# Strided attention heads on the 96-key blocks of the local heads: values on partitions 32 to 95

## Chip, cores and metric

One core of a Trainium2 chip runs the whole program in one launch. The metric is the time of one execution on the device in microseconds (us); the median of several runs is given, and beside it one execution that the profiler recorded.

## What is computed

The program is a causal sparse attention followed by two feed-forward stages (a mixture of experts with soft routing, then a gated layer). Only the attention is touched by the change:

```python
# B, H, S, D = 4, 8, 576, 64; stride 32
mask_local   = (rel >= 0) & (rel < stride)                            # heads 0 to 3
mask_strided = (rel >= 0) & (pos[None] % stride == pos[:, None] % stride)  # heads 4 to 7
scores = where(mask, scale * q @ k.T, -1e9);  attn = softmax(scores);  attn @ v
```

For a strided head the host stores the 576 positions in another order, residue by residue: 32 classes of 18 positions each. In that order a query sees only earlier keys of its own class of 18, so both kinds of head become a narrow band along the diagonal.

## The kernel before

**Units and tiles.** The attention is cut into 16 units, each a head for a pair of batch entries (`UNITS`, line 26). Their order is local, local, strided, strided, four times over, so units 2, 3, 6, 7, 10, 11, 14 and 15 are strided. A unit has nine query blocks of 64 rows. A local block looks at 96 keys (the 64 of its own block and the 32 before them), a strided one at 80 (the 64 and the 16 before). The widths are `WID = (96, 80)` on line 22; the key columns of a strided block begin 16 further on, by `SHIFT` on line 23.

**One unit.** `load_qk` (line 249) brings keys and queries, and `load_v` (line 254) the values: one DMA of 64 rows of 4680 bytes. It lands on partitions `W - 64` to `W`, that is 32 to 95 for a local head and 16 to 79 for a strided one. Then three copies on GpSimd (line 262) put the last `W - 64` rows of each block's predecessor onto partitions 0 to `W - 64`. The block's values are then `W` rows from partition 0. `qk` (line 274) makes the scores on TensorE (line 286); VectorE scales them, adds a mask (line 290) and takes the row maximum (line 291), in two parts of five and four blocks. `expo` (line 293) is the exponential on ScalarE, one instruction for each block. `tr` (line 298) transposes on TensorE (line 304) and copies on ScalarE (line 305). `pv` (line 307) multiplies with the values (line 321), and VectorE divides (lines 324 to 328). Every second unit, `xtr` (line 335) transposes the result again, and `logits` (line 345) multiplies it with the routing matrix.

**Order.** The order on each engine is written out by hand (line 594). Step n issues `qk(n)`, `tr(n-1)`, the exponentials of n, `pv(n-1)`, then the load of values n+1, then two weight loads of 512 KB each. Value tiles are two (`NV`), so the load of values n+1 waits for `pv(n-1)`; key tiles are three. All these loads are issued by SyncE and share one queue, so the packets of a load stand behind those of the loads issued before it. VectorE and ScalarE also convert some weights between the steps (`PRECONV`).

**Masks.** `h` is a piece of 96 columns of the constants' tile. `low` (line 525) fills it with two VectorE instructions; `cut` (line 517) compares it with a constant of each row and writes a mask in bf16. After step 0 `strided()` (line 534) fills `h` anew for 80 columns and makes the nine masks `ms` of the strided heads, before VectorE comes to the scores of unit 1. At about the same time GpSimd copies the values of unit 1 and zeroes the tile `eT` (line 544).

**After the attention** come the logits' end and the slots (lines 365 to 489), the expert layers (`w1_mm`, line 627, and line 719), for which the rest of the weights is loaded as buffers come free, and the gated layer (line 795 on).

Of the kernel before, what the change touches and what calls it, by code (L numbers as in the profile page):

```python
# [12 lines left out]
BF16 = mybir.dt.bfloat16  # L13
AF = mybir.ActivationFunctionType
ALU = mybir.AluOpType
# [3 lines left out]
HD = 64  # L19
NT = 9  # L20
PAD = 32
WID = (96, 80)
SHIFT = (0, 16)
NEG = -1.0e30
HORDER = (0, 1, 4, 5, 2, 3, 6, 7)
UNITS = [(bp, h) for bp in range(2) for h in HORDER]
# [49 lines left out]
def constants():  # L76
    p = np.arange(128)
    q = p % 64
    c = np.zeros((128, 16), np.float32)
    c[:, 0], c[:, 1], c[:, 2] = p, p % 32, p % 32 + 32 * (p // 64)  # L80
    c[:, 3], c[:, 4], c[:, 5], c[:, 15] = q, q + 32, q + 16, np.maximum(q, 31)
    for i in range(NT):
        c[:, 6 + i] = (64 * i + q) // 18 * 18 - 64 * i + 16
    return c


def layout(q, k, v, moe_phi, moe_w1, moe_w2, moe2_w_gate, moe2_w_val, moe2_w_out):
    pi = perm_index()
    kq = np.empty((16, 2, HD, 2, S), np.float32)
    vw = np.ones((16, 64, 2, NT, HD + 1), np.float32)  # L90
    for u, (bp, h) in enumerate(UNITS):
        y = h // 4
        o = pi if y else np.arange(S)
        kq[u, :, :, 0] = k[2 * bp:2 * bp + 2, h][:, o].transpose(0, 2, 1)
        kq[u, :, :, 1] = q[2 * bp:2 * bp + 2, h][:, o].transpose(0, 2, 1)
        vw[u, ..., :HD] = v[2 * bp:2 * bp + 2, h][:, o].reshape(2, NT, 64, HD).transpose(2, 0, 1, 3)
    w1 = moe_w1.reshape(8, 4, 128, 2, 512).transpose(0, 3, 2, 1, 4).reshape(16, 128, 2048)
    w2 = moe_w2.reshape(8, 2, 4, 128, 512).transpose(0, 1, 3, 2, 4).reshape(16, 128, 2048)
    g = bits(moe2_w_gate).reshape(4, 128, 12, 128)
    a = bits(moe2_w_val).reshape(4, 128, 12, 128)  # L100
    wgv = np.stack([g, a], axis=3).transpose(2, 1, 0, 3, 4).reshape(12, 128, 1024)
    wo = bits(moe2_w_out).reshape(6, 2, 128, 512).transpose(0, 2, 1, 3).reshape(6, 128, 1024)
    w1, w2 = (a.reshape(16, 128, 2, 1024).transpose(0, 2, 1, 3) for a in (w1, w2))
    wgv, wo = (a.reshape(-1, 128, 2, 512).transpose(0, 2, 1, 3) for a in (wgv, wo))
    phi = moe_phi.reshape(4, 128, 32).transpose(1, 0, 2).reshape(128, 128)
    arrs = dict(cst=constants(), phi=phi, kq=kq.reshape(16, 128, 2 * S),
                vh=vw.reshape(16, 64, -1),
                w1=w1, w2=w2, wgv=wgv, wo=wo)
    return {n: np.ascontiguousarray(x) for n, x in arrs.items()}
# [3 lines left out]
def build(ctx: ExitStack, tc: tile.TileContext, cst, phi, kq, vh, w1, w2, wgv, wo, out):  # L113
# [11 lines left out]
    lp = es_ld.enter_context(tc.tile_pool(name="ld", bufs=1, side="right"))  # L125
# [3 lines left out]
    def bank(tag, bufs):  # L129
        return pp[0].tile([128, 512], F32, tag=tag, name=tag, bufs=bufs)  # L130
# [17 lines left out]
    col = lp.tile([128, 128], F32, name="col")  # L148
    par = lp.tile([128, 16], F32, name="par")
    ml = lp.tile([128, 5, 96], BF16, name="ml")  # L150
    ms = lp.tile([128, 9, 80], BF16, name="ms")

    wsrc = [w1[j] for j in range(16)] + [w2[j] for j in range(16)]
    loads = [(j, hf) for j in PRE + WORDER for hf in range(2)]
# [99 lines left out]
    def load_v(u):  # L254
        if u >= 16:
            return
        W = WID[UNITS[u][1] // 4]
        t = vt[u % NV]
        SP.dma_start(out=t[W - 64:W], in_=vh[u])
        t4 = t.rearrange("p (b i d) -> p b i d", b=2, i=NT)  # L260
        for i0, i1 in ((1, 3), (3, 6), (6, 9)):
            POOL.tensor_copy(t4[0:W - 64, :, i0:i1, :], t4[64:W, :, i0 - 1:i1 - 1, :])  # L262

# [1 line left out]
    tmp = ap_.tile([128, 2880], F32, name="tmp")  # L265

    def etile(u):
        W = WID[UNITS[u][1] // 4]
        o = 864 * (u % 2)
        return tmp[:, o:o + NT * W].rearrange("p (j k) -> p j k", k=W)  # L270

    attile = tmp[0:96, 1728:2880].rearrange("p (j k) -> p j k", k=128)

    def qk(u):
        y = UNITS[u][1] // 4
        W = WID[y]
        e = etile(u)
        q, k = qbd[u % NQK], kt[u % NQK]
        mx = mxs[u] = ap_.tile([128, NT], F32, tag="mx", name="mx", bufs=2)
        for i0, i1 in zip(CUT, CUT[1:]):  # L280
            ps = bank("sc", 2)
            for i in range(i0, i1):
                c0 = 64 * i + SHIFT[y]
                for b in range(2):
                    h = slice(64 * b, 64 * b + 64)
                    PE.matmul(out=ps[h, W * (i - i0):W * (i - i0) + W], lhsT=q[h, 64 * i:64 * i + 64],  # L286
                              rhs=k[h, c0:c0 + W], start=True, stop=True, skip_group_check=True)
            p3 = ps[:, 0:(i1 - i0) * W].rearrange("p (j k) -> p j k", k=W)
            m3 = ms[:, i0:i1] if y else ml[:, i0:i1] if i0 == 0 else ml[:, 1:1 + i1 - i0]
            DVE.scalar_tensor_tensor(out=e[:, i0:i1], in0=p3, scalar=0.125, in1=m3, op0=ALU.mult, op1=ALU.add)  # L290
            DVE.tensor_reduce(out=mx[:, i0:i1], in_=e[:, i0:i1], axis=AX, op=ALU.max, negate=True)  # L291

    def expo(u, k):
        e, mx = etile(u), mxs[u]
        for i in range(CUT[k], CUT[k + 1]):
            ACT.activation(out=e[:, i], in_=e[:, i], func=AF.Exp, scale=1.0, bias=mx[:, i:i + 1])  # L296

    def tr(u):
        W = WID[UNITS[u][1] // 4]
        e = etile(u)  # L300
        for t in range(3):
            ps = bank("tr", 3)
            for j in range(3):
                PE.transpose(ps[0:W, 128 * j:128 * j + 128], e[:, 3 * t + j], ident)  # L304
            ACT.copy(attile[0:W, 3 * t:3 * t + 3], ps[0:W, 0:384].rearrange("p (j q) -> p j q", j=3))  # L305

    def pv(u):
        bp, h = UNITS[u]
        y = h // 4
        W = WID[y]  # L310
        st, e = divmod(h % 4, 2)
        if e == 0:
            xt[bp, y, st] = ap_.tile([128, NT, 128], F32, tag="x", name="x", bufs=6)
        x, v = xt[bp, y, st], vt[u % NV]
        dn = ap_.tile([128, 2, NT, 1], F32, tag="dn", name="dn", bufs=2)
        half = []
        for i0, i1 in zip(CUT, CUT[1:]):
            ps = bank("pv", 2)
            for i in range(i0, i1):
                for b in range(2):  # L320
                    PE.matmul(out=ps[64 * b:64 * b + 64, 65 * (i - i0):65 * (i - i0) + 65], lhsT=attile[0:W, i, 64 * b:64 * b + 64],  # L321
                              rhs=v[0:W, 65 * (NT * b + i):65 * (NT * b + i) + 65], start=True, stop=True, skip_group_check=True)
            p3 = ps[:, 0:65 * (i1 - i0)].rearrange("p (j d) -> p j d", d=65)
            DVE.tensor_scalar_add(dn[:, 0, i0:i1], p3[:, :, HD:HD + 1], 1.0e-9)
            half.append((i0, i1, p3))
        DVE.reciprocal(dn[:, 1], dn[:, 0])
        for i0, i1, p3 in half:
            DVE.tensor_tensor(out=x[:, i0:i1, 64 * e:64 * e + 64], in0=p3[:, :, 0:HD],
                              in1=dn[:, 1, i0:i1].to_broadcast([128, i1 - i0, HD]), op=ALU.mult)
# [169 lines left out]
    with tc.manual_schedule():  # L499
# [8 lines left out]
        ACT.dma_start(out=par, in_=cst)  # L508
        load_qk(0)
        load_v(0)  # L510
        load_qk(1)
        SP.dma_start(out=phi_t, in_=phi.rearrange("p (c s) -> p c s", c=4))
        load_half(WSCHED[0])
        load_v(1)
        load_qk(2)

        def cut(out, k, op, src):
            DVE.tensor_scalar(out=out, in0=src, scalar1=par[:, k:k + 1], scalar2=NEG, op0=op, op1=ALU.mult)
# [4 lines left out]
        h = cst_t[:, C_SEL4:C_SEL4 + 96]  # L523

        def low(n, k):
            DVE.tensor_scalar(out=h[:, 0:n], in0=col[:, 0:n], scalar1=par[:, k:k + 1], scalar2=-1000.0, op0=ALU.is_gt, op1=ALU.mult)
            DVE.tensor_tensor(out=h[:, 0:n], in0=h[:, 0:n], in1=col[:, 0:n], op=ALU.add)
# [4 lines left out]
        same(ident, 0, 128)  # L532

        def strided():
            low(80, 5)
            for i in range(NT):
                cut(ms[:, i], 6 + i, ALU.is_lt, h[:, 0:80])

        def sels():
            for g in range(4):  # L540
# [19 lines left out]
        for p in range(8):  # L560
            bp, y, st = p // 4, p % 2, p // 2 % 2
# [7 lines left out]
        for bp in range(2):  # L569
# [10 lines left out]
            else:  # L580
                at_late(b0, load_half, 2)
                at_late(b0 + 1, warm, WTAIL)
                for fn, *a in ((etr, 1, 0), (etr, 1, 1), (weights_a,), (slot, 1, 0, 0, 3), (etr, 1, 2),
# [3 lines left out]
                               (warm, WT[1])):  # L587
                    at_late(b0 + 2, fn, *a)
        at_late(0, strided)
        at_late(1, sels)  # L590
        for k, n in PRECONV:
# [347 lines left out]
        for n in range(len(seq) + LAG):  # L939
# [19 lines left out]
            while extra and (extra[0][0] <= room or n + 1 >= len(seq)):  # L959
                c, fn = extra.pop(0)  # L960
# [26 lines left out]
```

## Time and profile before

| | us |
|---|---|
| median of 3 runs | 363.52 |
| lowest and highest | 363.08, 364.82 |
| profiled execution, its own time | 362.7 |
| span of the profile, first to last instruction | 360.9 |

1.8 us of the profiled execution lie outside the span. The attention takes the first 96 us or so of the span, the slots go to 111, the expert layers to about 152, and the rest is the gated layer. The mean granted TensorE clock of the span is 0.991 of full speed. In the rows below, times are microseconds from the start of the span, and durations of single instructions are in nanoseconds where a row says "mean".

### The profile page before, as it was taken

How to read it: one execution, taken by the hardware profiler on the slowest of the kernel's cores; microseconds unless marked ns; L12 is line 12 of the kernel's file. 1: busy time of each engine (PE TensorE's matmuls, PEld its weight loads, DVE VectorE, ACT ScalarE, POOL GpSimd, SP SyncE). 2: the span in 40 equal slices, each digit the busy share in tenths (PEclk: the TensorE clock that was granted, in tenths of full speed). 3: DMA queues.
4: the chain of work that ended last, by engine and by line, in shares of the span. 5: the costliest groups of instructions: out<-in, count | busy, mean ns of one | idle time of the engine just before them, and what ended most of it. 6: DMA issues, size and time to landing. Idle time of an engine off the chain costs nothing.

```text
span 360.9 us, 7431 instructions
## 1 busy us (share of the span) xinstructions
PE 338.2 (94%) x2860; PEld 246.2 (68%) x2860; DVE 235.8 (65%) x487; ACT 193.5 (54%) x462; POOL 139.8 (39%) x147
## 2 busy tenths in 40 slices
PE   8899899899699999979998999999998999999995
PEld 4588688698475243337785767677685788888885
DVE  4998778968461045276886998999778824242442
ACT  1698968986630014157666655556455444453541
POOL 2213312213200020125666587347368654344431
PEclk9999999999999999987999999999999999999999
DMA  7999999997859999953140533333300003030321
GB/s 286 385 309 411 332 345 371 314 396 250 306 202 406 408 411 407 411 202 117 54 181 15 198 137 116 116 119 116 116 0 3 1 0 118 0 116 2 118 110 66
DMA packets 20804, 71.94 MB, mean 199 GB/s; under 512 B 2336, under 2 KB 2720, under 8 KB 20768
## 3 DMA queue, kind: packets, MB, share of 16 engines
q1 hardware_dynamic: 20624, 71.45, 54.3%
q8 instruction: 23, 0.38, 0.4%
q14 instruction: 13, 0.11, 0.1%
q10 hardware_dynamic: 144, 0.01, 0.0%
HBM read 66.73 MB, written 4.72 MB: 198 GB/s over the span
## 4 chain that ended last, share of the span: by engine, by line
PE 63%; DVE 11%; DMA 8%; ACT 6%; POOL 6%; issue 4%; DVEq 0%; POOLq 0%; ACTq 0%; SPq 0%
PE o L826 31%; PE pv L321 4%; PE sc L286 4%; PE gv L799 3%; DMA g<-in_wgv 3%; DMA wx<-in_w 3%; PE tr L304 3%; PE pv L719 3%; PE gv L800 2%; DMA v<-in_vh 2%; POOL hl L808 2%; POOL wol L770 2%; DVE h L806 2%; ACT tmp L296 2%; PE sc L630 2%
## 5 line engine op out<-in xcount | busy, mean ns | idle before, releaser
L808 POOL TENSOR_TENSOR hl<-h,hh 128x512 fp32r<-128x512 f32 (+1 forms) x60 | 72.3, 1206 | 91.0 <-ACT hh L807 90.9
L826 PE MATMUL o<-woh,hh 128*128 128x512 f32 (+1 forms) x222 | 86.7, 392 | 0.2 <-DVE acc L851 0.2
L826 PE MATMUL o<-wol,hh 128*128 128x512 f32 (+1 forms) x222 | 86.0, 389 | 0.0
L806 DVE TENSOR_TENSOR h<-gv,sg 128x512 f32<-128x512 f32 (+1 forms) x59 | 37.5, 636 | 56.0 <-ACT sg L805 42.6
L826 PE MATMUL o<-woh,hl 128*128 128x512 f32 (+1 forms) x222 | 66.8, 390 | 0.6 <-POOL hl L808 0.4
L807 ACT CAST hh<-h 128x512 fp32r<-128x512 f32 (+1 forms) x60 | 34.7, 578 | 54.6 <-DVE h L806 54.6
L826 PEld LDWEIGHTS o<-woh,hh 128*128 128x128 f32 x222 | 42.3, 190 | 10.1 <-DVE acc L851 0.6
L826 PEld LDWEIGHTS o<-woh,hl 128*128 128x128 f32 x222 | 41.8, 190 | 10.4 <-POOL hl L808 1.9
L262 POOL COPY v<-v 32x390 f32<-32x390 f32 (+3 forms) x48 | 22.8, 506 | 65.9 <-DMA v<-in_vh 47.6
L826 PEld LDWEIGHTS o<-wol,hh 128*128 128x128 f32 x222 | 42.3, 190 | 8.5
L296 ACT ACTIVATE tmp<-tmp,mx 128x96 f32<-128x96 f32 (+1 forms) x144 | 39.0, 358 | 11.9 <-DVE mx L291 11.9
L805 ACT ACTIVATE sg<-gv 128x512 f32<-128x512 f32 (+1 forms) x60 | 33.4, 557 | 20.2 <-PE gv L799 19.3
L286 PE MATMUL sc<-k 64*64 64x96 f32 (+1 forms) x576 | 26.1, 239 | 1.8 <-DVE tmp L290 1.6
L799 PE MATMUL gv<-cs,St 128*128 128x512 f32 (+1 forms) x60 | 25.8, 429 | 1.9 <-DVE St L788 1.9
L286 PEld LDWEIGHTS sc<-k 64*64 64x64 f32 x576 | 22.8, 133 | 4.9 <-DVE tmp L290 2.1
L321 PE MATMUL pv<-v,tmp 96*64 96x65 f32 (+1 forms) x576 | 22.7, 227 | 3.5 <-ACT tmp L305 2.2
L321 PEld LDWEIGHTS pv<-v,tmp 96*64 96x64 f32 (+1 forms) x576 | 19.8, 137 | 8.9 <-ACT tmp L305 7.6
L770 POOL TENSOR_TENSOR wol<-wo,woh 128x512 fp32r<-128x512 f32 x12 | 15.3, 1295 | 23.3 <-DMA g<-in_wgv 23.3
L305 ACT COPY tmp<-tr 96x384 f32<-96x384 f32 (+1 forms) x48 | 19.6, 477 | 6.9 <-PE tr L304 6.7
L800 PE MATMUL gv<-cs,St 128*128 128x512 f32 (+1 forms) x59 | 22.3, 379 | 0.2 <-DVE h L806 0.2
L304 PE MATMUL tr<-cst_t,tmp 128*96 128x128 f32 (+1 forms) x144 | 20.0, 280 | 1.9 <-ACT xT L340 1.9
L221 DVE SCALAR_TENSOR_TENSOR cv<-g,cv 128x512 int32<-128x512 int32 x30 | 20.8, 693 | 0.6
(159 smaller groups left out, 485.4 us busy)
## 6 DMA issues: line engine op xcount, KB each, us to landing
w<-in_w SPq DMA_DIRECT2D x56, 512.0 KB, 10.1
g<-in_wgv SPq DMA_DIRECT2D x10, 1024.0 KB, 4.8
k<-in_kq SPq DMA_DIRECT2D x16, 576.0 KB, 9.5
g<-in_wo SPq DMA_DIRECT2D x5, 1024.0 KB, 4.8
v<-in_vh SPq DMA_DIRECT2D x16, 292.5 KB, 7.4
out<-osb SPq DMA_DIRECT2D x17, 256.0 KB, 2.1
wx<-in_w SPq DMA_DIRECT2D x7, 512.0 KB, 10.1
w<-in_wgv SPq DMA_DIRECT2D x4, 512.0 KB, 6.9
```

What stands on the lines that cost most here:

```text
L262: POOL.tensor_copy(t4[0:W - 64, :, i0:i1, :], t4[64:W, :, i0 - 1:i1 - 1, :])
L286: PE.matmul(out=ps[h, W * (i - i0):W * (i - i0) + W], lhsT=q[h, 64 * i:64 * i + 64], rhs=k[h, c0:c0 + W], start=True, stop=True, skip_grou ...
L296: ACT.activation(out=e[:, i], in_=e[:, i], func=AF.Exp, scale=1.0, bias=mx[:, i:i + 1])
L304: PE.transpose(ps[0:W, 128 * j:128 * j + 128], e[:, 3 * t + j], ident)
L321: PE.matmul(out=ps[64 * b:64 * b + 64, 65 * (i - i0):65 * (i - i0) + 65], lhsT=attile[0:W, i, 64 * b:64 * b + 64], rhs=v[0:W, 65 * (NT * b ...
L799: PE.matmul(out=pg[:, 0:n], lhsT=St[f][:, 0:128], rhs=csf[:, t0:t0 + n], start=True, stop=True)
L800: PE.matmul(out=pvv[:, 0:n], lhsT=St[f][:, 128:256], rhs=csf[:, t0:t0 + n], start=True, stop=True)
L805: ACT.activation(out=sg[:, 0:n], in_=pg[:, 0:n], func=AF.Silu)
L806: DVE.tensor_tensor(out=h[:, 0:n], in0=pvv[:, 0:n], in1=sg[:, 0:n], op=ALU.mult)
L807: ACT.copy(hh[bi, f][:, 0:n], h[:, 0:n])
L808: POOL.tensor_tensor(out=hl[bi, f][:, 0:n], in0=h[:, 0:n], in1=hh[bi, f][:, 0:n].bitcast(F32), op=ALU.subtract)
L826: PE.matmul(out=o[:, 0:c], lhsT=(a, a, l)[i][:, 128 * t:128 * t + 128], rhs=(woh, wol, woh)[i][f][:, c * k:c * k + c], start=(first and i ...
```

## The change

All heads use blocks of 96 keys. The values of a strided head land on partitions 32 to 95, and GpSimd copies 32 rows to partitions 0 to 31, as for a local head. The key columns of a block begin 32 before it for both kinds. The first 16 of the 96 columns of a strided block are always masked: the row constants of the nine strided masks are 16 higher, and these masks are cut from the `h` that the local masks already use, so the two instructions of `low(80, 5)` are gone.

```diff
-WID = (96, 80)
-SHIFT = (0, 16)
+W = 96
@@ constants
-        c[:, 6 + i] = (64 * i + q) // 18 * 18 - 64 * i + 16
+        c[:, 6 + i] = (64 * i + q) // 18 * 18 - 64 * i + 32
@@ build
-    ms = lp.tile([128, 9, 80], BF16, name="ms")
+    ms = lp.tile([128, 9, 96], BF16, name="ms")
@@ load_v, etile, qk, tr, pv: the local W is gone
-        W = WID[UNITS[u][1] // 4]
@@ qk
-                c0 = 64 * i + SHIFT[y]
+                c0 = 64 * i
@@ strided
-            low(80, 5)
             for i in range(NT):
-                cut(ms[:, i], 6 + i, ALU.is_lt, h[:, 0:80])
+                cut(ms[:, i], 6 + i, ALU.is_lt, h)
```

## Rows read from the trace of the kernel before

**Rows 1.** The page's 40 slices of 9 us: DMA busy, bytes moved.

```profile
DMA  7999999997859999953140533333300003030321
GB/s 286 385 309 411 332 345 371 314 396 250 306 202 406 408 411 407 411 202 117 54 181 15 198 137 116 116 119 116 116 0 3 1 0 118 0 116 2 118 110 66
```

**Rows 2.** The chain of waits at the end of the expert layers: start, us, what.

```profile
140.97 10.96 DMA g<-in_wgv
```

**Rows 3.** Windows of 3 us: busy PE, PEld, DVE, ACT, POOL, then PEclk, DMA share, GB/s.

```profile
33.00:36.00 3.00, 3.00 (x59) 2.62 (x57) 2.88 (x9) 2.49 (x10) 0.52 (x2) 1.00 1.01 411
38.00:41.00 3.00, 3.00 (x80) 2.43 (x72) 2.54 (x9) 3.00 (x12) 0.33 (x1) 1.00 1.02 273
```

**Rows 4.** Issue of the values of unit 6, and its landing, by the tile v.

```profile
L259 SPq DMA_DIRECT2D v<-in_vh x1: 515/515/515, 34.2 to 34.2; - x1
...
DMA to landing us min/median/max: 9.0/9.0/9.0
```

**Rows 5.** Timeline of PE: start, us, instruction, count, [idle before and its releaser].

```profile
32.52 1.63 PE L321 MATMUL pv<-v,tmp 96*64 96x65 f32 x36
...
38.45 1.27 PE L321 MATMUL pv<-v,tmp 96*64 96x65 f32 x36
39.66 1.46 PE L286 MATMUL sc<-k 64*64 64x80 f32 x36
...
43.34 1.94 PE L321 MATMUL pv<-v,tmp 80*64 80x65 f32 x36 [1.11 <-DMA v<-in_vh]
...
46.34 1.70 PE L286 MATMUL sc<-k 64*64 64x96 f32 x36
...
49.70 1.75 PE L321 MATMUL pv<-v,tmp 80*64 80x65 f32 x36
...
54.14 1.76 PE L321 MATMUL pv<-v,tmp 96*64 96x65 f32 x36
...
65.55 1.42 PE L321 MATMUL pv<-v,tmp 80*64 80x65 f32 x36 [1.39 <-ACT tmp L305]
```

**Rows 6.** Timeline of POOL: copies of the values of unit 6.

```profile
43.35 1.30 POOL L262 COPY v<-v 16x260 f32<-16x260 f32 x3 [5.01 <-DMA v<-in_vh]
```

**Rows 7.** Timeline of DVE in the mask build, and five compares of another mask later.

```profile
9.77 0.25 DVE L526 TENSOR_SCALAR cst_t<-col,par 128x80 f32<-128x80 f32 x1
...
10.33 1.12 DVE L518 TENSOR_SCALAR ms<-cst_t,par 128x80 bf16<-128x80 f32 x6
...
11.36 2.31 DVE L518 TENSOR_SCALAR ms<-cst_t,par 128x80 bf16<-128x80 f32 x1
...
13.80 0.64 DVE L290 SCALAR_TENSOR_TENSOR tmp<-sc,ml 128x480 f32<-128x480 f32 x1
...
17.34 0.83 DVE L521 TENSOR_SCALAR cst_t<-col,par 128x32 f32<-128x32 f32 x5
```

**Rows 8.** Timeline of POOL at the same time.

```profile
11.24 1.37 POOL L262 COPY v<-v 32x260 f32<-32x260 f32 x3 [4.50 <-DMA v<-in_vh]
12.56 1.05 POOL L544 MEMSET eT<- 128x1152 f32 x1
```

**Rows 9.** Timeline of PE just after the mask build.

```profile
14.50 0.91 PE L286 MATMUL sc<-k 64*64 64x80 f32 x20 [1.34 <-DVE tmp L290]
15.65 0.77 PE L286 MATMUL sc<-k 64*64 64x80 f32 x16 [0.24 <-DVE tmp L290]
...
18.63 1.41 PE L321 MATMUL pv<-v,tmp 96*64 96x65 f32 x36 [0.60 <-ACT tmp L305]
```

**Rows 10.** Groups by line and shape in the attention: count, busy us, mean ns, idle before.

```profile
L296 ACT ACTIVATE tmp<-tmp,mx 128x96 f32<-128x96 f32 x72 | 20.0, 364 | 10.5 <-DVE mx L291 10.5
L296 ACT ACTIVATE tmp<-tmp,mx 128x80 f32<-128x80 f32 x72 | 19.0, 352 | 1.5 <-DVE mx L291 1.4
...
L290 DVE SCALAR_TENSOR_TENSOR tmp<-sc,ml 128x480 f32<-128x480 f32 x8 | 5.2, 651 | 0.8 <-PE sc L286 0.8
...
L290 DVE SCALAR_TENSOR_TENSOR tmp<-sc,ms 128x400 f32<-128x400 f32 x8 | 4.5, 563 | 0.0
```

More of the change, by code (lines that the diff above doesn't have):

```diff
@@ L267, in etile @@
     def etile(u):
-        W = WID[UNITS[u][1] // 4]
         o = 864 * (u % 2)
@@ L275, in qk @@
         y = UNITS[u][1] // 4
-        W = WID[y]
         e = etile(u)
@@ L298, in tr @@
     def tr(u):
-        W = WID[UNITS[u][1] // 4]
         e = etile(u)
@@ L309, in pv @@
         y = h // 4
-        W = WID[y]
         st, e = divmod(h % 4, 2)
```

## The prediction

> **What bounds the kernel now.** Start with the page's 40 slices [rows 1]: through the attention (the first ten) the DMA row stands at 9 nearly everywhere, yet the bytes moved swing between 250 and 411 GB/s. The engines of the DMA are busy all the time and not always effective. Two windows show when [rows 3]: at 33 to 36 us, while values of a local head (unit 5) land, 411 GB/s; at 38 to 41, before the strided values of unit 6 land, 273. The share is 1.01 and 1.02. So a load onto partitions 16 to 79 slows the whole queue. Next the landing of one such load [rows 4]: issued at 34.2, 9.0 us later in place, at 43.2. Then TensorE's timeline [rows 5], the engine that sets the pace of the steps: most products with the values take 1.27 us without a gap, as at 38.45. At 43.34 the product waits 1.11 us for these very values and then takes 1.94, because GpSimd's copies [rows 6] follow the landing and release it piece by piece. Those at 32.52, 49.70 and 54.14 are stretched too.
>
> There is a second stall early on. VectorE makes the strided masks from 10.33 us; six run smoothly, the seventh begins at 11.36 and takes 2.31 us [rows 7]. GpSimd is busy from 11.24 to 13.61 with two unrelated jobs [rows 8]. The scores of unit 1 begin on VectorE only at 13.80, and TensorE waits 1.34, 0.24 and 0.60 us [rows 9].
>
> What the attention gains reaches the end nearly whole: the DMA idles in the slots (202 GB/s in the slice at 99 us [rows 1]) until the end of the attention frees buffers, then moves 406 to 411 GB/s until about 153 us [rows 1], and a load issued at 140.97 is on the chain for 10.96 us [rows 2]. Earlier buffers mean an earlier end of that stretch.
>
> **Term 1, the values' landing place.** The strided loads become like the local ones. In the 38 to 41 window 3 x (1 - 273/411) = 1.0 us was lost; I take 1.0 as the least per strided load. Units 2, 3 and 6 then give the values of unit 6 at least 3 us: landing 40.2, copies done 41.5, wanted at 43.34 - 1.11 = 42.23. A step moves 2 x 512 + 576 + 292.5 KB = 1.94 MB, 4.7 us at 411 GB/s, no more than TensorE's step (from the product at 32.52 to the one four steps later at 54.14 pass 21.62 us; less the stalls between, 0.36 + 1.78 + 0.48, that is 4.75 a step), so the queue does not fall behind again. The stalls that go: 1.63 - 1.27 = 0.36 (unit 4), 1.11 + 1.94 - 1.27 = 1.78 (unit 6), 0.48 (unit 7), 0.49 (unit 8) [rows 5]: **-3.1 us**. Bounds: 0, if the slow windows have another cause, and 3.3, with the 0.15 that unit 10's product at 65.55 is longer; I take 3.1, the sum that the rows give. What is late next there is ScalarE: that product waits 1.39 us for it, whatever the values do.
>
> [...]
>
> **Term 2, wider scores.** TensorE's 36 records of a strided unit go from 1.46 to the local 1.70 us [rows 5]: +0.24 a unit. VectorE's first part goes from 563 to 651 ns [rows 10], +0.09; the reduction behind it reads the same elements and is put at the same, and the second part of four blocks at four fifths: +0.32 a unit. ScalarE: 9 x 12 ns = +0.11. On the path: units 2, 3, 6, 7, 10 and 14 by TensorE, 6 x 0.24 = 1.44. Unit 11's scores lie in front of the 1.39 us wait at 65.55 and are hidden; without that cover they cost 0.24. Unit 15 is last, nothing runs beside it, and its chain is VectorE, then ScalarE: 0.09 + 0.09 + 0.11 = 0.29. Sum **+1.7 us**; bounds 0 (all in the shade of waits) and 8 x 0.32 = 2.6 (VectorE everywhere).
>
> Costed at nothing: transposes and value products (their count of columns stays, 96 rows take the same 1.27 as others), GpSimd's copies (32 rows as in local heads; they lie between landing and product, and at 0.1 us more would still end before 42.2), SyncE's queue (the same issues, the same waits). The change adds no wait.
>
> **Term 3, the masks.** Two instructions fall out ahead of the nine: they began at 9.77, the first mask at 10.33. Now the first mask can begin at 9.77. Its pitch: six take 1.12 with the last 0.26, so (1.12 - 0.26)/5 = 0.172 at 80 columns; the five compares of mostly 32 columns give (0.83 - 0.24)/4 = 0.148 [rows 7]. That is 0.5 ns a column, so 0.180 at 96. The ninth begins at 9.77 + 8 x 0.180 = **11.21**, and GpSimd began at 11.24 [rows 8]. The sixth of before, at 11.19, got through; the one at 11.36 did not. It is a close race, which I take as just won. Then the scores of unit 1 begin at 11.21 + 0.18 = 11.4 rather than 13.80, 2.4 earlier, and TensorE sheds its waits of 1.34 + 0.24 + 0.60: **-2.2 us** (bounds 0 and 2.4). The values of unit 2 are then wanted 2.2 us earlier too, and term 1 brings them at least 1.0; if the slack is short, up to 1.2 of the gain stays behind as a wait there, which the range has to hold.
>
> [...]
>
> **Sum.** -3.1 + 1.7 - 2.2 = -3.6. The profiled execution took 362.7, of which 360.9 is span, so it would take 359.1; it stands 0.8 below the median of 363.5, which becomes **360.0**.
>
> **Rivals.**
> *B, the race is lost.* The ninth mask starts after GpSimd's first copy (a landing 0.05 us earlier is enough, or 1 ns a column: pitch 0.189, start 11.28) and waits until 13.6 as before. VectorE gains at most 0.2. For it: the margin of 0.03 us. Against: a pitch from two rows. 363.5 - 3.1 + 1.6 - 0.2 = 361.8.
> *C, the gain is given back.* With the values early, ScalarE paces the steps (the wait for it at 65.55 exists now, and exponentials are 20.0 + 19.0 us of its time [rows 10]), half of term 1 returns, and the race is lost: 363.5 - 1.55 + 1.7 - 0.2 = 363.4.
> *D, slower.* The windows at 273 GB/s are slow for a reason other than the landing place, so the values are late as before; VectorE's longer instructions then stand at the head of every strided step: 363.5 + 2.6 - 0.2 = 365.9. It decides if the rate with strided values stays near 273. Against: unit 5 and unit 6 differ in nothing but partitions, and move at 411 and 273.
> *E, the change doesn't do what it says.* Partitions of the load are fixed by its slice; I give this nothing beyond D.
>
> **Chances.** The forecast 0.47, B 0.30, C 0.16, D 0.07. Half a per cent is 1.8 us, about what a measurement of this kernel can tell from no change: faster means below 361.7. Nearly all of the forecast, somewhat under half of B and little of C lie there: 0.60. Slower (above 365.3) is most of D: 0.06. The rest, 0.34, is no difference. The range takes in the forecast with term 1 and term 3 at their better bounds and cheaper scores, 358.8, and B and most of C, 363.4; the likeliest case alone spans 358.8 to 361.2.
>
> **What would show it.** Windows with strided values at about 400 GB/s, landings under 8 us, and products at 43 us without a gap and 1.27 long confirm term 1; 1.70 us for all scores term 2. In the mask build, nine instructions of equal length and the scores of unit 1 near 11.4 mean the race is won; one of about 2 us means B. The prediction is wrong if the products with values still wait for the DMA, or if these waits turn up under ScalarE's name.

## The result, and the profile after

The changed kernel takes **358.88 us** (median of 12 runs, 357.10 to 361.41); the kernel before, run beside it, 363.90 (12 runs, 361.57 to 365.81). The ratio is 0.9867, 95% interval 0.9836 to 0.9898: 4.8 us less (3.7 to 6.0). The forecast was 360.0, 3.5 less, with a range of 358.8 to 363.4. The profiled execution took 358.82 us, of which 356.9 is span, at a mean granted clock of 0.990 (before: 0.991), so this pair of profiles can be set side by side.

The page of the changed kernel, its slices of 8.9 us and the loads of values (median us from issue to landing last):

```profile
PEclk9999999999999999978999999999999999999999
DMA  7999999966679999933332433333300003030331
GB/s 288 409 407 407 391 378 388 376 220 242 241 290 416 408 411 406 409 139 115 118 119 85 150 119 118 118 120 118 118 1 2 1 0 119 0 118 2 119 116 62
...
v<-in_vh SPq DMA_DIRECT2D x16, 292.5 KB, 5.5
```

The swings between 250 and 411 GB/s of [rows 1] are gone from the second slice to the eighth (376 to 409); after it, from 71 us on, the digit of DMA is 6 where it was 9, 7 and 8: the queue now runs dry (a share of 0.64 from 71 to 80 us) and waits for buffers (from 71 to 89 us the issues of values wait three times for a product with values, 12.1 us in all; before, 11.4 us, with the share still at 0.97 from 73 to 82), where the kernel waited for the queue (1.11 us at 43.34 in [rows 5]). A load of values lands after 5.5 us in the median (7.4 before); in both profiles the 69 loads issued in the first 95 us land in the order of their issue. The two windows of [rows 3], for the changed kernel, with the same columns:

```profile
33.00:36.00 3.00, 2.41 (x43) 2.08 (x42) 2.93 (x8) 3.00 (x12) 1.50 (x3) 1.00 1.03 410
38.00:41.00 3.00, 3.00 (x60) 2.72 (x55) 2.79 (x9) 3.00 (x11) 1.31 (x3) 1.00 1.07 403
```

The second moves 403 GB/s where it moved 273. The values of unit 6, which answer to [rows 4], by the tile v:

```profile
L257 SPq DMA_DIRECT2D v<-in_vh x1: 515/515/515, 32.0 to 32.0; - x1
...
DMA to landing us min/median/max: 7.0/7.0/7.0
```

Issued at 32.0, landed at 39.0; the prediction put the landing at 40.2. TensorE's timeline, which answers to [rows 5] and to the last line of [rows 9]:

```profile
15.84 1.41 PE L315 MATMUL pv<-v,tmp 96*64 96x65 f32 x36 [0.33 <-ACT tmp L300]
...
26.59 1.27 PE L315 MATMUL pv<-v,tmp 96*64 96x65 f32 x36
...
30.54 1.41 PE L315 MATMUL pv<-v,tmp 96*64 96x65 f32 x36
...
37.14 1.27 PE L315 MATMUL pv<-v,tmp 96*64 96x65 f32 x36
38.34 1.70 PE L282 MATMUL sc<-k 64*64 64x96 f32 x36
41.22 1.40 PE L315 MATMUL pv<-v,tmp 96*64 96x65 f32 x36
...
47.12 1.27 PE L315 MATMUL pv<-v,tmp 96*64 96x65 f32 x36
...
51.07 1.40 PE L315 MATMUL pv<-v,tmp 96*64 96x65 f32 x36
...
62.36 1.42 PE L315 MATMUL pv<-v,tmp 96*64 96x65 f32 x36 [1.44 <-ACT tmp L300]
```

In this execution no product with values waits for the DMA any more, and none takes more than 1.42 us. What is left is ScalarE's wait at unit 10 (1.44 us; 1.39 before), as the prediction said of that unit. A second profile of the changed kernel (group 2 below) still has one such wait, of 0.19 us at unit 2, with a product of 1.94 us:

```profile
20.23 1.94 PE L315 MATMUL pv<-v,tmp 96*64 96x65 f32 x36 [0.19 <-DMA v<-in_vh]
```

The strided scores take 1.70 us. The mask build, on VectorE and then on GpSimd, which answers to [rows 7, 8]:

```profile
9.37 1.70 DVE L512 TENSOR_SCALAR ms<-cst_t,par 128x96 bf16<-128x96 f32 x9
10.98 0.65 DVE L286 SCALAR_TENSOR_TENSOR tmp<-sc,ml 128x480 f32<-128x480 f32 x1
...
11.09 1.30 POOL L260 COPY v<-v 32x260 f32<-32x260 f32 x3 [4.40 <-DMA v<-in_vh]
12.35 1.05 POOL L537 MEMSET eT<- 128x1152 f32 x1
```

Nine masks in one run of 1.70 us, done before GpSimd begins at 11.09; the scores of unit 1 begin at 10.98 instead of 13.80.

**Where the 4.0 us of span went.** Subtract the starts of the products with values, unit by unit: unit 1 is 2.79 us earlier than before (15.84 against 18.63), unit 5 only 1.31 (37.14 against 38.45), unit 9 3.19 (56.90 against 60.09), and the end of unit 15, 92.91 against 95.76, is 2.85 earlier. So the masks' stall gives first, units 2 to 5 take half of it back (the wider scores of units 3 and 6 explain 0.48 of the 1.48; ScalarE is busy without a break in the window at 33), and the stalls of units 6 to 8 then give 1.9. The expert layers add about 0.8: their first layer ends at 124.61 against 128.23, 3.6 earlier, and the gated layer most of the rest, 0.3 (from the first of its last products to the end of the span pass 199.99 us against 200.29). Not all of the first number is the change's: the product of unit 0, which the change doesn't touch, came at 11.39 against 11.79, 0.40 earlier by the start of the execution alone. In the expert layers the first layer's products wait three times for weights (`wx`, at 117.76, 120.31 and 122.88) in the kernel before and twice (116.68, 119.26) in the changed one, 0.22 to 0.25 us each; why one wait less, and whether it makes the 0.8, was not tried.

### The profile page after: what moved, and what is told of

It is laid out like the page before. It is cut to its first block, busy times and chain, and to the rows that moved or that the text cites. A ratio compares the mean times of both kernels' runs of the same rounds, so it can differ in the third digit from the quotient of the medians.

```text
span 356.9 us, 7428 instructions
## 1 busy us (share of the span) xinstructions
PE 337.2 (94%) x2860; PEld 247.3 (69%) x2860; DVE 236.4 (66%) x485; ACT 194.7 (55%) x462; POOL 140.9 (39%) x147
## 4 chain that ended last, share of the span: by engine, by line
PE 53%; DVE 16%; DMA 12%; ACT 7%; POOL 6%; issue 5%; DVEq 0%; POOLq 0%; ACTq 0%
PE o L819 31%; DMA w<-in_w 9%; ACT tmp L292 4%; DMA wx<-in_w 3%; PE gv L792 3%; PE pv L315 3%; PE sc L282 3%; PE gv L793 3%; POOL hl L801 2%; DVE mx L287 2%; PE tr L299 2%; POOL wol L763 2%; DVE h L799 2%; DVE tmp L286 2%; DVE wg L224 2%
## 5 line engine op out<-in xcount | busy, mean ns | idle before, releaser
L260 POOL COPY v<-v 32x390 f32<-32x390 f32 (+1 forms) x48 | 23.9, 530 | 61.4 <-DMA v<-in_vh 52.0
L292 ACT ACTIVATE tmp<-tmp,mx 128x96 f32<-128x96 f32 x144 | 40.0, 362 | 10.0 <-DVE mx L287 9.9
L282 PE MATMUL sc<-k 64*64 64x96 f32 x576 | 27.8, 246 | 0.4 <-issue 0.2
L282 PEld LDWEIGHTS sc<-k 64*64 64x64 f32 x576 | 24.4, 133 | 3.0 <-issue 1.7
L315 PEld LDWEIGHTS pv<-v,tmp 96*64 96x64 f32 x576 | 19.3, 137 | 6.4 <-ACT tmp L300 6.1
L315 PE MATMUL pv<-v,tmp 96*64 96x65 f32 x576 | 21.3, 225 | 1.9 <-ACT tmp L300 1.8
L300 ACT COPY tmp<-tr 96x384 f32<-96x384 f32 x48 | 19.7, 477 | 4.9 <-PE tr L299 4.8
L299 PE MATMUL tr<-cst_t,tmp 128*96 128x128 f32 x144 | 19.9, 280 | 2.3 <-ACT xT L334 2.2
```

## The experiments

The result lies just inside the range, 0.1 us from its lower end, so the question is whether the three terms are what made it. The account tested is the prediction's: the landing place is worth 3.1 us, the masks 2.2, the wider scores cost 1.7, and they add. The rival account is that the race of the masks has little to do with the change, and that the landing place carries all of the gain and more. Each ratio is against runs of the kernel before beside it on the same chip, whose median was 366.01 (first group), 365.13 (second) and 365.13 (third).

| kernel | median us | ratio to before | 95% interval | group |
|---|---|---|---|---|
| after, values on 16 to 79 again | 365.30 | 0.9954 | 0.9918 to 0.9990 | 1 |
| before, values on 32 to 95 | 357.59 | 0.9788 | 0.9742 to 0.9834 | 1 |
| after, two instructions back | 360.21 | 0.9837 | 0.9798 to 0.9875 | 1 |
| before, two instructions gone | 364.25 | 0.9950 | 0.9919 to 0.9981 | 1 |
| after, unchanged | 360.46 | 0.9854 | 0.9813 to 0.9894 | 2 |
| before, 32 to 95 and instructions gone | 358.39 | 0.9810 | 0.9775 to 0.9846 | 2 |
| after, strided scores 80 wide | 359.20 | 0.9821 | 0.9784 to 0.9858 | 2 |
| after, GpSimd's work put later | 359.69 | 0.9846 | 0.9807 to 0.9885 | 2 |
| before, idle products | 366.30 | 1.0033 | 0.9991 to 1.0074 | 3 |
| after, 18 products of warm-up | 361.41 | 0.9898 | 0.9847 to 0.9948 | 3 |

**The changed kernel with the strided values on partitions 16 to 79.** Everything else of the change stays.

```diff
-        SP.dma_start(out=t[32:96], in_=vh[u])
+        lo = 16 if UNITS[u][1] // 4 else 32
+        SP.dma_start(out=t[lo:lo + 64], in_=vh[u])
```

> The kernel after, but the values of a strided unit land on partitions 16 to 79 again; the copies and the products read rows 0 to 95 as before, so a part of a strided unit's values is left over from an earlier unit, and the widths, the masks and all waits are those of the kernel after. Theory 1 (the landing place sets the rate of the whole queue, and its worth is the stalls that it made): windows with strided values fall back from about 400 to about 300 GB/s, and TensorE waits for values again at units 6 to 8; about 3 us more than the kernel after, some 362 us. Theory 2 (with the values early another engine paces the steps, the landing place is worth little): the rate falls, but the time rises by 1 us or less. Theory 3 (the rate has nothing to do with the partitions): about 400 GB/s, no change in time.

Measured: 0.9954, 1.7 us less than before (0.4 to 3.0), where the change gives 0.9867 and 0.9854. Its page, and its products of units 1 to 3 on TensorE's timeline:

```profile
GB/s 265 394 301 351 329 359 390 284 403 255 335 170 413 408 408 408 410 234 116 9 181 43 172 176 116 116 118 116 116 0 3 1 0 117 0 116 2 117 109 67
```

```profile
15.95 1.41 PE L316 MATMUL pv<-v,tmp 96*64 96x65 f32 x36 [0.23 <-ACT tmp L301]
21.97 1.94 PE L316 MATMUL pv<-v,tmp 96*64 96x65 f32 x36 [0.94 <-DMA v<-in_vh]
...
31.14 2.17 PE L316 MATMUL pv<-v,tmp 96*64 96x65 f32 x36
```

The slices swing as in [rows 1]. The waits are not at units 6 to 8, where they were expected: unit 6's product, at 45.90, takes 1.40 us without a wait. The masks ran here without a stall, and the product of unit 1 came at 15.95, as early as in the changed kernel (15.84). But unit 2 now waits 0.94 us for its values and takes 1.94, and unit 3 comes at 31.14, against 26.59 in the changed kernel. Of these 4.6 us the clock has some 0.6, an estimate: the granted clock was at half from 29.73 us (0.53 in the window from 29.5 to 33.0), and the products from 29.27 to 31.14 took 0.82 and 1.19 us, against 0.71 and 0.69 at full clock in a profile of the kernel before. Most of what the early masks gave has turned into a wait for values, and two units on nothing of it is left: unit 3 comes later than the 28.56 of the kernel before.

**The kernel before with its strided values on 32 to 95**, and nothing else.

```diff
-        SP.dma_start(out=t[W - 64:W], in_=vh[u])
+        SP.dma_start(out=t[32:96], in_=vh[u])
```

> The kernel before with one edit: the values of a strided unit land on partitions 32 to 95; the 80-key products then read rows that don't fit their keys, and the work is otherwise the same. Theory 1: about 400 GB/s with strided values, no wait of TensorE for values, 2.5 to 3.3 us less than the kernel before, about 361 us, with the stall of VectorE in the mask build still there. Theory 2: 1 us or less. Theory 3: no change.

Measured: 0.9788, that is 7.8 us less than before, more than the whole change. Its page, and VectorE and GpSimd in the mask build:

```profile
GB/s 259 413 409 409 409 410 412 343 216 259 223 337 416 407 410 408 409 109 110 118 120 118 118 120 118 118 121 118 118 1 2 1 0 120 0 118 2 120 118 61
```

```profile
8.75 0.24 DVE L527 TENSOR_TENSOR cst_t<-cst_t,col 128x80 f32<-128x80 f32 x1
9.03 1.63 DVE L518 TENSOR_SCALAR ms<-cst_t,par 128x80 bf16<-128x80 f32 x9
...
11.74 1.31 POOL L262 COPY v<-v 32x260 f32<-32x260 f32 x3 [3.59 <-DMA v<-in_vh]
```

409 to 413 GB/s from the second slice to the seventh: one changed line, the partitions of the load, does that, and rival D falls. And a surprise: with both instructions of `low` still there, the masks were done 1.1 us before GpSimd began.

**The two instructions, put back into the changed kernel and taken out of the kernel before.**

```diff
+            low(96, 4)
             for i in range(NT):
                 cut(ms[:, i], 6 + i, ALU.is_lt, h)
```

> The kernel after with the two small VectorE instructions ahead of the nine masks put back; they write the same numbers again, so what is computed is the same. Theory 1 (the masks won a race against GpSimd): the masks begin about 0.55 us later, the last of them start after GpSimd's copy, one mask takes about 2 us again, and the time rises by about 2 us to some 361. Theory 2 (no race; the stall had another cause and went with the values): two instructions, about 0.5 us more or nothing. Theory 3 (race, but later steps are paced elsewhere and give the gain back): the stall is in the trace, and the time rises by less than 1 us.

```diff
-        c[:, 6 + i] = (64 * i + q) // 18 * 18 - 64 * i + 16
+        c[:, 6 + i] = (64 * i + q) // 18 * 18 - 64 * i + 32
...
-            low(80, 5)
...
-                cut(ms[:, i], 6 + i, ALU.is_lt, h[:, 0:80])
+                cut(ms[:, i], 6 + i, ALU.is_lt, h[:, 16:96])
```

> The kernel before with the masks cut from columns 16 to 95 of the mask row that the local heads use, and the two instructions ahead of them left out; widths and landing place are those of before and the result is the same. Theory 1: nine masks of equal length, the scores of unit 1 on VectorE near 11.3 us, and up to 2.2 us less than the kernel before; as the values of strided units still land late, the gain may run into that wait and shrink to 1 us or less. Theory 2 (no race): 0.5 us or less, one mask still takes about 2 us.

Measured: 0.9837 with them back, which is not told from the changed kernel's own 0.9867 and 0.9854; 0.9950 for the kernel before without them, 1.8 us less (0.7 to 3.0). In the profile of the first, on VectorE and GpSimd:

```profile
8.85 0.26 DVE L520 TENSOR_SCALAR cst_t<-col,par 128x96 f32<-128x96 f32 x1
9.14 0.26 DVE L521 TENSOR_TENSOR cst_t<-cst_t,col 128x96 f32<-128x96 f32 x1
9.44 1.70 DVE L512 TENSOR_SCALAR ms<-cst_t,par 128x96 bf16<-128x96 f32 x9
...
11.37 1.31 POOL L260 COPY v<-v 32x260 f32<-32x260 f32 x3 [4.39 <-DMA v<-in_vh]
```

The two cost 0.59 us, from 8.85 to 9.44, and the ninth mask still begins before 11.37 (9.44 + 8 x 0.18 = 10.88). With them in, the race can be won. In the profile of the second the masks ran without a stall too, from 9.33 to 10.95, ahead of GpSimd's copies at 11.27.

**Two more executions of the kernel before** ask how often its race is lost.

> The kernel before, unchanged, a second look. The profiled execution of the forecast took 362.7 us at a mean granted clock of 0.991; the other executions of the kernel before had 0.975 to 0.990, a median of 0.981, and took 1 to 5 us longer. Theory 1 (waits for strided values make the granted clock fall to half for some microseconds, now here, now there): this look shows clock rows at 0.5 inside the attention, after a wait for values, products and transposes in them that take up to twice as long, and the masks' stall may be there or not. Theory 2 (the executions differ in something outside the attention): the attention is as in the first profile, and the clock falls elsewhere.

> The same as the run above, a third look, for how often the masks' stall and the half clock occur. Theory 1: half clock inside the attention in at least one of the two looks. Theory 2: in none.

Measured: 364.51 and 364.56 us. In the first the race was won, in the second lost. VectorE in the first, then TensorE's products of units 1 to 3:

```profile
9.47 1.63 DVE L518 TENSOR_SCALAR ms<-cst_t,par 128x80 bf16<-128x80 f32 x9
11.01 0.65 DVE L290 SCALAR_TENSOR_TENSOR tmp<-sc,ml 128x480 f32<-128x480 f32 x1
```

```profile
15.87 1.41 PE L321 MATMUL pv<-v,tmp 96*64 96x65 f32 x36 [0.44 <-ACT tmp L305]
...
21.43 1.47 PE L321 MATMUL pv<-v,tmp 80*64 80x65 f32 x36
...
27.76 0.71 PE L304 MATMUL tr<-cst_t,tmp 128*80 128x128 f32 x5 [1.52 <-issue]
...
29.02 1.27 PE L321 MATMUL pv<-v,tmp 80*64 80x65 f32 x36
```

Against the profile of before that the prediction read, unit 1 is 2.76 us earlier (15.87, 18.63), unit 2 1.30 (21.43, 22.73) and unit 3 0.46 *later* (29.02, 28.56). The whole 2.8 us of the race is gone two units on. The row at 27.76 waits 1.52 us under the name "issue"; the values of unit 3 had landed at 26.64, and in the changed kernel with values on 16 to 79 the same row waits 2.02 and begins about 1.0 us after that landing too. The profile does not name the values there, so this link is argued; that the gain goes when the values land on 16 to 79, and stays when they land on 32 to 95, is measured.

The second lost the race and still waited at unit 6. VectorE, then TensorE:

```profile
10.60 3.63 DVE L518 TENSOR_SCALAR ms<-cst_t,par 128x80 bf16<-128x80 f32 x9
14.15 0.64 DVE L290 SCALAR_TENSOR_TENSOR tmp<-sc,ml 128x480 f32<-128x480 f32 x1
```

```profile
45.90 1.94 PE L321 MATMUL pv<-v,tmp 80*64 80x65 f32 x36 [1.98 <-DMA v<-in_vh]
```

What differs between won and lost is the start of the execution. By the trace's clock records, which begin with the rise, the granted clock rose to full (1.00) at 6.5 and 7.0 us in the two profiles of before that lost the race, and the 12 products of warm-up, 0.43 us apart until then, ended at 6.35 and 6.36; it rose at 4.6 in the one that won it, where the last ones came 0.22 apart and ended at 5.57. VectorE's masks follow that start; GpSimd's copies follow a load, and begin at 11.1 to 11.7 in all profiles named so far.

**A race made to be lost.** First with GpSimd's zeros and copies of unit 1 put behind a tiny copy that waits for the first row maxima:

```diff
+                if n == 0:
+                    POOL.tensor_copy(ap_.tile([128, 5], F32, name="mark"), mxs[0][:, 0:5])
+                    POOL.memset(eT, 0.0)
+                    copies(1)
```

> The kernel after with GpSimd's zeros of eT and its copies of the values of unit 1 put behind a tiny copy of the first row maxima, so that GpSimd is busy when VectorE makes the strided masks, in every execution. Theory 1 (the two engines lock each other out and it counts): some masks take 1 to 2 us, the scores of unit 1 begin on VectorE about 2 us later than at 11.0 us, and the time rises by some 2 us. Theory 2 (the lock is real, but later steps are paced by values or by another engine): the stall is there and the time rises by 0.7 us or less. Theory 3 (no lock): nine masks of equal length.

This failed as a test: it made no stall (0.9846). The profile on VectorE and GpSimd:

```profile
9.69 1.71 DVE L516 TENSOR_SCALAR ms<-cst_t,par 128x96 bf16<-128x96 f32 x9
...
8.98 1.06 POOL L595 MEMSET eT<- 128x1152 f32 x1
12.09 1.30 POOL L256 COPY v<-v 32x260 f32<-32x260 f32 x3 [2.04 <-DMA v<-in_vh]
```

The zeros run from 8.98 to 10.04 and the masks from 9.69 on, in 1.71 us in all. The zeros held VectorE for the little that was left of them: the first mask alone, in a narrow window, is

```profile
9.69 0.42 DVE L516 TENSOR_SCALAR ms<-cst_t,par 128x96 bf16<-128x96 f32 x1
```

It took 0.42 us instead of 0.26 and ended 0.07 us after the zeros, as the mask at 11.36 in [rows 7] ended 0.06 after GpSimd's last job; the others followed at their usual pitch. The copies then came after the masks. This execution started late (the clock rose at 6.2, the warm-up ended at 6.35, as in the lost races of before), and the ninth mask, 8 x 0.18 after 9.69, began at 11.1, ahead of the 11.24 of [rows 8]; but its own copies had been moved away, so it is no race won. Second, with a longer warm-up, which moves all of TensorE and VectorE against the loads:

```diff
-WARM0 = 12
+WARM0 = 18
```

> The kernel after with 18 instead of 12 idle products at its start, so that TensorE, and VectorE's masks behind it, come about 1.4 us later, while the values of unit 1 land when they did: the masks begin near 10.8 us and GpSimd's copies at 11.1 to 11.6. Theory 1 (the race is real, as in the first profile of the kernel before): one or two masks take about 2 us, the scores of unit 1 begin near 14 us, and the time rises by about 3 us against the kernel after. Theory 2 (the stall in that profile was an accident of another kind): nine equal masks, and the time rises by 1.4 us or less.

Measured: 0.9898. VectorE, GpSimd and unit 1 on TensorE:

```profile
11.36 3.66 DVE L512 TENSOR_SCALAR ms<-cst_t,par 128x96 bf16<-128x96 f32 x9
14.95 0.64 DVE L286 SCALAR_TENSOR_TENSOR tmp<-sc,ml 128x480 f32<-128x480 f32 x1
...
11.53 1.31 POOL L260 COPY v<-v 32x260 f32<-32x260 f32 x3 [4.03 <-DMA v<-in_vh]
12.79 1.05 POOL L537 MEMSET eT<- 128x1152 f32 x1
...
19.79 1.41 PE L315 MATMUL pv<-v,tmp 96*64 96x65 f32 x36 [0.60 <-ACT tmp L300]
```

Here the stall is back: 3.66 us for nine masks, and unit 1 at 19.79, against 15.89 in a profile of the unchanged kernel. 2.4 of these 3.9 us are the longer warm-up itself (unit 0 at 13.39 against 11.00); the stall is the other 1.5, since from unit 0 to unit 1 pass 6.40 instead of 4.89. No product with values waits for the DMA afterwards, and the attention ends at 96.25 against 92.56, 3.7 later. So in this pair of profiles, where the values are early, a loss at the start is carried through to the end of the attention, which in the kernel before a gain at the start was not. By the spans the two stand 3.1 apart (359.3, 356.2), by the ratios 1.6 (0.9898 - 0.9854), with intervals that overlap; so what the stall alone is worth here is not told from nothing.

**The sum by parts.** The changed kernel once more; the kernel before with 32 to 95 and without the two instructions, which is the change without its wider scores; and the changed kernel with strided scores, masks and exponentials 80 columns wide in columns 16 to 95 of the block, the first 16 zeroed by GpSimd.

> The kernel after, unchanged, beside the next three on one chip. In the first session it took 0.987 of the kernel before, while the landing place alone, in another session, took 0.979. If the widths cost what the prediction put on them (1.7 us, half a per cent), it lies 0.005 above the landing place alone, about 0.984; if the two sessions' chips differ, the ratio here tells by how much.

```diff
-        SP.dma_start(out=t[W - 64:W], in_=vh[u])
+        SP.dma_start(out=t[32:96], in_=vh[u])
...
-            low(80, 5)
```

> The kernel before with strided values landing on partitions 32 to 95 and with the two mask instructions gone, the widths still 80; the strided products read rows that don't fit their keys. Theory 1 (the three terms, widths +1.7 us): 1.7 us less than the kernel after. Theory 2 (the widths lie in the shade of ScalarE and VectorE): as the kernel after within 0.7 us. Theory 3 (wider scores also lengthen VectorE's and ScalarE's work at every step, which now sets the pace): 2.5 to 3 us less.

```diff
+                if n + 1 < 16 and UNITS[n + 1][1] // 4:
+                    POOL.memset(etile(n + 1)[:, :, 0:16], 0.0)
...
-                c0 = 64 * i
+                c0 = 64 * i + z
```

> The kernel after with strided scores, masks and exponentials 80 columns wide again, in columns 16 to 95 of blocks that stay 96 wide; GpSimd writes zeros to the first 16 columns, a strided unit's instruction of some 0.2 us, and transposes and products keep 96 rows, so the result is that of the reference. Theory 1: the widths' 1.7 us come back, about 2 us below the kernel after. Theory 2: no difference within 0.7 us. Theory 3: 2.5 to 3 us below. If GpSimd's zeros delay the copies of the values or the scores, TensorE waits for POOL in the trace and the gain is less.

Measured: 0.9854, 0.9810, 0.9821. From the second to the first, the wider scores cost 0.0044 x 365.13 = 1.6 us; from the third to the first, 1.2. The intervals overlap, so neither alone is told from nothing. The traces say the same from another side: from the start of the product of unit 5 to the end of the attention pass 55.93 us in the changed kernel (36.63 to 92.56), 55.03 and 54.71 in the other two. That is 0.9 and 1.2 for the scores of units 7, 10, 11, 14 and 15 (those of unit 6 run ahead of unit 5's product), for which the prediction has 3 x 0.24 + 0.29 = 1.0. The version with 80 columns leaves nothing out, and its median is below the changed kernel's beside it (359.20, 360.46), but the two are not told apart.

**Idle products ahead of the products with values**, in units 2, 3, 6 and 7 of the kernel before, to see whether the late values cost more than their waits by letting TensorE's clock fall.

```diff
+                if n - 1 in (2, 3, 6, 7):
+                    wbank[:] = "pv", 2
+                    warm(4)
+                    wbank[:] = "tr", 3
```

> The kernel before with four idle products (zeros, 512 columns, about 1 us in all, their result unused) on TensorE ahead of the products with values of units 2, 3, 6 and 7, so that TensorE has work while it waits for these values. Theory 1: the clock falls less often inside the attention, a mean granted clock of 0.985 or more instead of 0.981; the idle products cost up to 1 us a unit where nothing is waited for, so the time lies between 2 us less and 2 us more than the kernel before. Theory 2: the clock stays at 0.981 and the time rises by 1 to 4 us.

Measured: 1.0033, no gain. The median of the mean granted clock was 0.9835, against 0.981 of the kernel before beside it, less than expected. This is inconclusive: the products cost time themselves, and the clock hardly moved.

## Why the prediction was right, and where it was wrong

**The sign, the range and the traces' steps hold; that the sum came near is luck.** Windows with strided values at 403 GB/s, the landing of unit 6 at 39.0 (40.2 predicted), its product without a gap, scores at 1.70, nine masks of equal length, the scores of unit 1 at 10.98 (11.4 predicted): all as written under what would show it. Its sign of being wrong, a product with values that still waits for the DMA, shows once, with the 0.19 us at unit 2 of the second profile. The pitch of the masks is (1.70 - 0.26)/8 = 0.180 us, as worked out from the rows.

**Term 1 was mis-sized: 3.1 us, at most 3.3, where the runs show more.** The partitions of the load are worth 7.8 us on the kernel before (0.9788), 5.1 on the one without the two instructions (0.9950 to 0.9810, across groups) and 3.7 on the changed kernel (0.9954 to 0.9854, across groups). The step that failed is "the stalls that go", taken as the sum of the stalls in one profile: that profile had the lost race in it, and its 2.4 us gave the values of units 2 and 3 time to land. Unit 3's product began there at 28.56, the very moment its copies ended. Without the lost race the late values stall units 2 and 3 instead. A stall that another one covers has no row. The prediction saw this ("if the slack is short"), but took it for a loss of term 3, where it is a gain of term 1. Nor are all the rows that it summed the landing place's: in the changed kernel the products of units 4 and 8 still take 1.41 and 1.40 us, not 1.27, and unit 4's took 1.63 in its second profile, as before.

Why a load onto partitions 16 to 79 is slower than one onto 32 to 95, no run shows; what the runs show is the rate of the queue: 273 GB/s in the slow window of [rows 3] with the first, 403 in the same window of the changed kernel, and 409 to 413 from the second slice to the seventh of the kernel before with that one edit.

A second part of the excess goes with the clock, less firmly. The profile of before that the prediction read was at 0.991; the executions of that kernel beside the experiments had a median of 0.981, the kernels with values on 32 to 95 0.986 to 0.995. In one execution of the kernel before, that of 364.51 us, three windows of 4 us show it:

```profile
62.00:66.00 4.00, 1.90 (x29) 1.48 (x23) 3.81 (x11) 2.74 (x9) 0.29 (x1) 1.00 1.01 285
66.00:70.00 4.00, 3.88 (x42) 3.61 (x41) 2.42 (x9) 3.61 (x12) 1.01 (x3) 0.51 1.05 271
70.00:74.00 4.00, 4.00 (x46) 3.66 (x45) 3.07 (x9) 0.90 (x3) 1.08 (x3) 0.64 1.01 326
```

In the first TensorE is busy 1.90 of 4 us (its product of unit 10 began at 65.70, right after its values landed at 65.56); then the granted clock stood at half for 6.8 us (0.51 and 0.64 in the next two windows). The prediction priced waits alone. That late values bring this about is not shown: behind unit 10's product the clock also fell, for 3.4 us, in three profiles with the values on 32 to 95 (the kernel before with that one edit, the changed kernel with the two instructions back and with GpSimd's work put later). Executions at one mean clock narrow it: in the first group those at 0.990 took 364.3 and 364.5 us for the kernel before and 357.1, 359.5 and 359.6 for the one with values on 32 to 95. That is 5.6 us on the mean, still above the bound of 3.3, and leaves some 2 of the 7.8 to the clock, by five executions.

**Term 2 holds:** 1.7 predicted, 1.6 and 1.2 by ratios, and 0.9 to 1.2 where 1.0 was due by the traces; neither ratio by itself is told from nothing. (Rival B's sum has 1.6 for it without saying why; with 1.7 it is 361.9.)

**Term 3 was right alone and wrong in the sum.** The stall exists, as [rows 7, 8] show and the longer warm-up repeats. But the kernel before does not always have it: with the two instructions in, the race was lost in the two executions that started late, and won in four others (the kernel before, the same with idle products, the same with 32 to 95, and the changed kernel with them back). Without them it was won in all six profiles with the copies in their place and the short warm-up, the clock rising at 4.2 to 5.8 us; none of these started as late as the two that lost, and the longer warm-up lost it. Taking them out is worth 1.8 us on the kernel before, and nothing that can be told once the values are early (0.9788 with, 0.9810 without; 0.9837 with, 0.9867 and 0.9854 without). The step that failed is the sum: terms 1 and 3 were added, and each wait stands behind the other. Together they were put at -3.1 - 2.2 = -5.3 us, and the kernel before with both measures 6.9 us less (0.9810, that is 5.6 to 8.2), of which the place alone already gives 7.8 and the masks alone 1.8. So the rival account, that the landing place carries the gain and more, comes nearer than the prediction's. From 6.9 the wider scores take 1.6 and leave 5.3 for the change beside it (this is no check: the 1.6 is that difference); the first measurement gave 4.8. The forecast of 3.5 came near because the price of the masks, which had no place beside term 1, filled a part of what term 1 lacked. That is luck.

What holds VectorE in the stall, no run shows; how long it is held, the runs show. VectorE sat out three copies and the zeros in a row (2.31 us for one mask in [rows 7], 2.39 and 2.37 in the two other profiles with the stall), each time to 0.05 to 0.08 us after the zeros' end, and beside the zeros alone a mask was held to 0.07 after their end. So in these profiles the stall lasted as long as GpSimd's work came without a gap. That it always does is not shown: earlier in the profile of before GpSimd made three copies from 5.32 to 6.75 us, and a mask begun at 5.70 ended at 6.38, ahead of the third copy's end. What tells the two apart is open.

**The rivals.** B, the race lost, did not come about, and its premise, one outcome for one kernel, does not hold for the kernel before, which lost it in two of three profiles. C's mechanism is there in part: units 2 to 5 give back 1.5 us and ScalarE is the wait at unit 10; it does not undo the gain. D is refuted by the rate.

**Open:** the 0.8 us in the expert layers; the wait named "issue" at unit 3; and how much of term 1 is waits and how much the clock, since the idle products didn't tell and five executions at one clock are few.

## What to carry to other kernels

Read a DMA queue by bytes moved at full busy share, not by the share: where two loads of the same size differ in rate, look at the partitions on which they land (here 411 and 273 GB/s, at shares of 1.01 and 1.02). Add up the stalls of one profile only after asking of each what it gave time to: a stall that goes may uncover another that no row shows (here 0.94 us at unit 2, in the changed kernel with values on 16 to 79), and two that cover each other do not add (here 7.8 and 1.8 us alone, 6.9 together). Where two engines meet within tenths of a microsecond, take several executions of the same kernel before giving the meeting a price (here one profile of three won the race).

## What the runs showed of the hardware

The granted clock is a part of the spread between executions of one kernel, about 1.5 us in the pair of windows below. After a wait of 1.7 us for ScalarE at unit 10, one execution kept full clock and another did not. The window around that wait, in the changed kernel with the two instructions back:

```profile
61.00:65.50 4.50, 3.45 (x43) 3.32 (x44) 3.88 (x11) 4.46 (x15) 1.30 (x3) 0.67 0.97 374
```

and in the changed kernel itself:

```profile
61.00:65.50 4.50, 3.47 (x69) 3.23 (x71) 4.28 (x12) 4.46 (x15) 1.31 (x3) 1.00 0.99 388
```

TensorE's busy time (3.45 and 3.47 us) and its wait (1.68 and 1.67) are the same and the clock is 0.67 against 1.00; the next product with values comes 9.06 us after the one of unit 10 in the first (62.05 to 71.11) and 7.59 in the second (62.03 to 69.62). So one such stretch costs about 1.5 us. A second place is the start of the gated layer, where the clock was at half for 3.4 us in some executions and 6.8 in others, kernel before and changed kernel alike: from the first of its last products to the end of the span pass 199.1 to 199.6 us in the first kind and 200.0 to 200.9 in the second. That 1 us came with either kernel, and a comparison of two single profiles can carry it.
